# Chunk results turned by VectorE and scaled by a spread row, in a sketched-attention and squared-ReLU kernel

## The chip, the cores and the metric

The kernel runs on one core of one Trainium2 chip. The metric is the time of one execution on the device in microseconds (us). TensorE (PE in the profile) multiplies matrices, VectorE (DVE) and ScalarE (ACT) work element by element and read the matmul results, GpSimd (POOL) works on the on-chip memory only, and SyncE (SP) issues nearly all DMAs. Each engine takes its own instructions in order; semaphores tie the engines together.

## What is computed

Attention with a polynomial sketch comes first, then a feed-forward layer with a squared ReLU. Cut to what matters:

```
phi(x) = outer(S1 x, S2 x)                # 8 x 8 = 64 features for each token and head
kv  = phi(k)^T v ;  z = sum phi(k)        # for each batch and head
x   = (phi(q) kv) / (phi(q) z + 1e-6)     # B*S = 4 * 1088 tokens, H*D = 128 wide
out = relu(x @ w_in)^2 @ w_out            # 128 -> 2048 -> 128, float32
```

The output has 4352 rows of 128 float32, one row for each token.

## The kernel before

**The chunks.** Each of the 4 batches has 1088 tokens: 1024 are cut into two groups of 512 (g = 0, 1), and the 64 that remain are put together over the batches. The feed-forward layer runs over ten chunks in this order: batch 0's first group as two halves of 256 tokens; then (0,1), (1,0), (1,1), (2,0), (2,1), (3,0), of 512 tokens each, (b,g) being batch and group; then the 256 remaining tokens; and (3,1) at the end. For a chunk, `x` is kept transposed and in 16 bits (`xT`, features on partitions, tokens along the free axis). `normalize` (lines 416 to 478) divides each token's 128 values by their largest, so that they fit 16 bits, and leaves the square of that factor in `beta`, a tile of 128 partitions x 4 with token 128 t + p at partition p, column t. GpSimd writes `beta` (line 468).

**One block.** `block` (line 694) does one of 16 slices of the hidden layer: a matmul into `pg` (line 679), the ReLU on ACT into `gt` (line 686), the square on VectorE into `g2` (line 687; the profile names the tile `g`), and two blocks later the matmul that adds into `po` (line 706). `po` is [128 features x 512 tokens]. The tiles `po` have two buffers in PSUM, and so have `pg` and the tiles tagged `ms`.

**The end of a chunk.** `po` has features on the partitions and the output has tokens as rows. So `to_tokens` (line 617) copies `po` to `oT` on ACT (line 620), and two blocks later TensorE transposes it in four 128 x 128 matmuls against the identity into `o_ps` (line 624). `store` (line 648) scales on VectorE with `beta`, one scale for each partition and group of 128 columns, into `o_sb` (line 653), and issues the stores on SP (line 661). For chunk (0,1), whose tokens lie as TensorE transposed them, that is one DMA; for the other five it is four, each with runs of 512 bytes. The last chunk has its own way (lines 715 and 637) and is not touched.

**The other work.** Attention for the next chunks is written as generators (`q_gen`, `k_gen`, and so on), which `pump` advances between blocks. In each batch's turn of the main loop (line 791) there are 16 blocks while `q_gen(b, 1)` and `k_gen(b+1)` run, then the loads for batch b+2 are issued (lines 806 to 813), then 16 blocks while `q_gen(b+1, 0)` runs. The loads of k, v and q of batch b+2 are `pinned`: each stays behind whatever DMA was written just before it for SP. v comes in 32 small DMAs with runs of 128 bytes (line 110). Two tiles of k and of q for the batches 2 and 3 are transposed in blocks of 32 x 32 by VectorE (`turned`, line 237). Up to line 789 the order of the work is written out by hand; behind that, all instructions that are not pinned are put in order for each engine at build time, by what they depend on and by planned times, and so an instruction of a later generator can stand well ahead of its place in the code. At run time the order on an engine is fixed.

Of the kernel before, what the change touches and what calls it, by code (L numbers as in the profile page):

```python
# [8 lines left out]
F32 = mybir.dt.float32  # L9
# [3 lines left out]
def _v(t: bass.AP, off: int, free, p0: int = 0, n: int = 128):  # L13

    p = list(t.ap)[0]
    return bass.AP(
        t.tensor, t.offset + p0 * p[0] + off, [[p[0], n]] + [list(d) for d in free]
    )
# [3 lines left out]
def kernel(  # L22
# [11 lines left out]
    nc = tc.nc  # L34

    B, H, S, D = 4, 4, 1088, 32
    DFF, NC = 2048, 16
    E = 128
    NJ = 8
# [4 lines left out]
    mult = mybir.AluOpType.mult  # L44
# [6 lines left out]
    apool = ctx.enter_context(tc.tile_pool(name="attn", bufs=2))  # L51
    fpool = ctx.enter_context(tc.tile_pool(name="ffn", bufs=3))
    pspool = ctx.enter_context(
        tc.tile_pool(name="psm", bufs=2, space=bass.MemoryType.PSUM)
    )

    def evict(eng, dst, src):
# [422 lines left out]
    chunks = []  # L480
    BY_PE = ((0, 1), (B - 1, 1))

    def chunk_of(b, g, xT, beta):
        at = out.offset + (b * S + 4 * g) * E
        if (b, g) in BY_PE:
            dsts = [(bass.AP(out.tensor, at, [[NJ * E, 128], [1, 512]]), 0, 128, 0, 512)]
        else:
            dsts = [
                (
                    bass.AP(  # L490
                        out.tensor, at + j * E, [[NJ * E, 32], [32 * NJ * E, 4], [1, E]]
                    ),
                    32 * j, 32, 0, 512,
                )
                for j in range(4)
            ]
        chunks.append((xT, 4, [(beta, 4)], dsts))

    def half_gen(phT, t0, m, tag, bufs):

# [8 lines left out]
    def x_gen(b, g, phT, m=32):  # L509
        nd = numerators(b, phT, m)  # L510
        yield 1
        xT = apool.tile([128, 512], F16, name="xT", tag="xT", bufs=3)
        beta = yield from normalize(nd, 4, xT, 0)
        chunk_of(b, g, xT, beta)
        yield 1
# [101 lines left out]
    def to_tokens(po, nt):  # L617

        oT = fpool.tile([128, 512], F32, tag="oT", bufs=2)
        nc.scalar.copy(oT[:, 0:nt], po[:, 0:nt])  # L620
        yield 2
        o_ps = pspool.tile([128, 512], F32, tag="ms", bufs=2)
        for t in range(nt // 128):
            nc.tensor.transpose(  # L624
                o_ps[:, 128 * t : 128 * t + 128], oT[:, 128 * t : 128 * t + 128], iden[:, :]
            )
        return o_ps

    def store_gen(po, nt, betas, dsts):
        o_ps = yield from to_tokens(po, nt)  # L630
        store(o_ps, betas, dsts)

# [15 lines left out]
    def store(po, betas, dsts):  # L648

        o_sb = fpool.tile([128, 512], F32, tag="o_sb", bufs=2)  # L650
        t0 = 0
        for beta, n in betas:
            nc.vector.tensor_tensor(  # L653
                out=_v(o_sb, 128 * t0, [[128, n], [1, 128]]),
                in0=_v(po, 128 * t0, [[128, n], [1, 128]]),
                in1=_v(beta, 0, [[1, n], [0, 128]]),
                op=mult,
            )
            t0 += n
        for dst, p0, n, c0, w in dsts:  # L660
            nc.sync.dma_start(dst, _v(o_sb, c0, [[E, w // E], [1, E]] if n == 32 else [[1, w]], p0, n))

    LOOK = 2
    LAST = 9
# [27 lines left out]
    po = [None]  # L692

    def block():
# [29 lines left out]
        if c0 + n == NC:  # L724
            if ci < LAST:
                stores.append([store_gen(po[0], nt, *chunks[ci][2:]), now[0]])
                pump_stores()
            else:
                _, _, [(beta, _)], [(dst, _, _, _, _)] = chunks[ci]
                store_last(po, beta, dst)  # L730
# [126 lines left out]
```

## Time and profile before

| what | us |
|---|---|
| runs of the kernel before | 213.95, 214.51, 216.04 (median 214.51) |
| the profiled execution: its own time | 213.53 |
| the profiled execution: span of the trace | 211.4 |
| TensorE busy | 201.1 |
| VectorE busy | 145.3 |
| ScalarE busy | 111.7 |
| GpSimd busy | 46.7 |

The span runs from the first to the last instruction in the trace; 2.1 us of the profiled execution's own time lie around it. The granted clock of TensorE is full throughout. In the chain of work that ended last, each line is the piece of work that released the next one; a piece of TensorE work in it can only be shortened by doing less of it or by doing it sooner. In a timeline, brackets give the idle time of an engine before an instruction and what ended it. SPq is SyncE's sequencer, where a DMA's issue takes time.

### The profile page before, as it was taken

The page shows a single profiled execution, that of the slowest core. Times are in us where ns is not written, and L with a number is a line of the kernel's source. Part 1 is how long each engine was busy: PE and PEld are TensorE (multiplying, and loading weights), DVE is VectorE, ACT ScalarE, POOL GpSimd, SP SyncE. Part 2 cuts the span into 40 slices and gives each one's busy share as a digit, 9 for nine tenths or more (in the row PEclk, how much of TensorE's full clock was granted, in tenths as well). Part 3 has the DMA queues.
Part 4 walks back from the last instruction along what each step waited for, and adds up shares of the span by engine and source line. Part 5 has one row for each costly group of instructions (what it writes and reads, how often), then busy time and mean ns, then how long its engine had stood idle before and what let it go on. Part 6 is the DMA issues. An engine that isn't in the chain of part 4 may idle for free.

```text
span 211.4 us, 5449 instructions
## 1 busy us (share of the span) xinstructions
PE 201.1 (95%) x2241; PEld 125.6 (59%) x2241; DVE 145.3 (69%) x281; ACT 111.7 (53%) x212; POOL 46.7 (22%) x66
## 2 busy tenths in 40 slices
PE   7887999899999999999999999999999899999993
PEld 6665778664644544555545555455445454789992
DVE  3667677836586899867777657567858777766662
ACT  3466664254556455455455553655565456555550
POOL 1002174104040683004130971022102210000000
PEclk9999999999999999999999999999999999999999
DMA  6999101422400421231000200001000100010001
GB/s 173 234 349 300 19 2 39 121 34 31 136 0 0 140 47 29 33 110 50 3 2 2 54 3 3 0 15 38 0 0 5 47 3 0 2 50 16 12 0 50
DMA packets 25736, 11.36 MB, mean 54 GB/s; under 512 B 13296, under 2 KB 25328, under 8 KB 25712
## 3 DMA queue, kind: packets, MB, share of 16 engines
q1 hardware_dynamic: 25632, 11.02, 19.8%
q8 instruction: 17, 0.28, 0.6%
q14 instruction: 7, 0.06, 0.1%
q10 hardware_dynamic: 80, 0.01, 0.0%
HBM read 8.79 MB, written 2.23 MB: 52 GB/s over the span
## 4 chain that ended last, share of the span: by engine, by line
PE 84%; DMA 7%; DVE 5%; SPq 2%; issue 1%; ACT 0%; DVEq 0%
PE po L706 47%; PE pg L679 14%; PE po L716 7%; DMA t<-in_k_dram 4%; PE nd L204 4%; PE ab_ps L204 3%; PE t_ps L376 3%; DVE g L687 3%; DMA v_first<-in_v_dram 2%; PE kv_ps L299 2%; PE o_ps L624 2%; PE xt_ps L218 1%; SPq L79 1%; PE x_ps L474 1%; SPq L149 1%
## 5 line engine op out<-in xcount | busy, mean ns | idle before, releaser
L687 DVE TENSOR_TENSOR g<-gt 128x512 f32<-128x512 f32 x136 | 101.6, 757 | 45.6 <-ACT gt L686 42.8
L706 PE MATMUL po<-g,w_o 128*128 128x512 f32 (+1 forms) x288 | 123.4, 525 | 1.2 <-DVE g L687 1.2
L686 ACT ACTIVATE gt<-pg 128x512 f32<-128x512 f32 x136 | 81.2, 599 | 48.3 <-PE pg L679 46.7
L706 PEld LDWEIGHTS po<-g,w_o 128*128 128x128 f32 x288 | 52.3, 191 | 26.3 <-issue 8.8
L241 POOL TENSOR_TENSOR ph<-ab 128x512 f32<-128x512 f32 (+1 forms) x27 | 32.7, 1238 | 62.5 <-ACT ab L59 62.5
L679 PE MATMUL pg<-xT,w_in 128*128 128x512 f16 x112 | 42.5, 381 | 0.0
L679 PEld LDWEIGHTS <-w_in 128*128 128x128 f16 x160 | 15.6, 99 | 20.3 <-issue 16.7
L465 POOL TENSOR_SCALAR mp<-mm 128x4 f32<-128x4 f32 (+2 forms) x11 | 5.3, 487 | 60.3 <-DVE mm L445 60.3
L716 PEld LDWEIGHTS po<-w_o,g 128*128 128x128 f32 x128 | 16.6, 191 | 0.6
L716 PE MATMUL po<-w_o,g 128*128 128x128 f32 x128 | 16.6, 275 | 0.0
L59 ACT COPY sb<-t_ps 128x512 f32<-128x512 f32 (+1 forms) x18 | 9.1, 516 | 9.9 <-PE t_ps L376 9.8
L59 ACT COPY ab<-ab_ps 128x256 f32<-128x256 f32 (+1 forms) x19 | 6.3, 339 | 12.9 <-PE ab_ps L204 11.3
L204 PEld LDWEIGHTS ab_ps<-w_bd,xt 128*32 128x32 f32 (+1 forms) x476 | 8.9, 113 | 6.6 <-issue 3.8
L204 PE MATMUL ab_ps<-w_bd,xt 128*32 128x64 f32 (+1 forms) x476 | 12.1, 224 | 0.2 <-ACT xt L59 0.2
L204 PEld LDWEIGHTS nd<-kvbd,sb 128*32 128x32 f32 x480 | 8.0, 110 | 6.3 <-issue 4.0
L376 PEld LDWEIGHTS t_ps<-iden,ph 128*128 128x128 f32 x60 | 7.5, 141 | 6.8 <-issue 4.9
L204 PE MATMUL nd<-kvbd,sb 128*32 128x66 f32 x480 | 9.9, 222 | 0.9 <-issue 0.9
L477 ACT COPY xT<-x_ps 128x512 f16<-128x512 f16 x7 | 4.1, 586 | 9.9 <-PE x_ps L474 9.9
L376 PE MATMUL t_ps<-iden,ph 128*128 128x128 f32 x60 | 9.2, 272 | 0.0
L59 ACT COPY xt<-xt_ps 128x512 f32<-128x512 f32 (+1 forms) x11 | 5.1, 471 | 6.0 <-PE xt_ps L218 6.0
L653 DVE TENSOR_TENSOR o_sb<-o_ps,beta 128x512 f32<-128x512 f32 (+2 forms) x10 | 5.5, 555 | 3.1 <-PE o_ps L624 2.9
L679 PE MATMUL pg<-xT_h,w_in 128*128 128x256 f16 x32 | 6.0, 273 | 0.9 <-ACT gt L686 0.5
(70 smaller groups left out, 117.2 us busy)
## 6 DMA issues: line engine op xcount, KB each, us to landing
t<-in_k_dram SPq DMA_DIRECT2D x3, 512.0 KB, 4.1
t<-in_q_dram SPq DMA_DIRECT2D x3, 512.0 KB, 4.1
out_dram<-o_sb SPq DMA_DIRECT2D x20, 64.0 KB, 1.8
w_in<-in_moe_w_in_dram SPq DMA_DIRECT2D x2, 512.0 KB, 5.7
w_o<-in_moe_w_out_dram SPq DMA_DIRECT2D x2, 512.0 KB, 7.9
v_turned<-in_v_dram SPq DMA_DIRECT2D x64, 16.0 KB, 1.7
k_sb<-in_k_dram SPq DMA_DIRECT2D x2, 256.0 KB, 3.0
q_sb<-in_q_dram SPq DMA_DIRECT2D x2, 256.0 KB, 5.4
```

What stands on the lines that cost most here:

```text
L59: return nc.scalar.copy(dst, src)
L204: nc.tensor.matmul(out_ps[p0 + c : p0 + c + m, c0 : c0 + w], lhsT[:, l0 + c : l0 + c + m], rhs,)
L241: eng.tensor_tensor(out=_v(ph, 256 * t0, [[64, 4 * w], [8, 8], [1, 8]]), in0=_v(ab, 64 * t0, [[16, 4 * w], [1, 8], [0, 8]]), in1=_v(ab, 64 ...
L299: nc.tensor.matmul(self.ps[c : c + self.m, at : at + w], _v(ph, c0 + 128 * pr + c, [[1, self.m]], p0, n), v_of(2 * pr + c // 64), start=c ...
L376: nc.tensor.transpose(t_ps[:, 128 * t : 128 * t + 128], ph[:, 256 * t + 128 * pr : 256 * t + 128 * pr + 128], iden[:, :],)
L465: nc.gpsimd.tensor_scalar(out=mp[:, 0:T], in0=mm[:, 0:T], scalar1=1.0 / 1024.0, scalar2=None, op0=mult)
L653: nc.vector.tensor_tensor(out=_v(o_sb, 128 * t0, [[128, n], [1, 128]]), in0=_v(po, 128 * t0, [[128, n], [1, 128]]), in1=_v(beta, 0, [[1, n ...
L679: nc.tensor.matmul(pg[:, nt * i : nt * i + nt], w_in[:, 128 * (c + i) : 128 * (c + i) + 128], xT[:, 0:nt],)
L686: nc.scalar.activation(gt[:, :], pg[:, :], Relu)
L687: nc.vector.tensor_tensor(out=g2[:, :], in0=gt[:, :], in1=gt[:, :], op=mult)
L706: nc.tensor.matmul(po[0][:, 0:nt], w_o[:, 128 * c : 128 * c + 128], g2[:, nt * i : nt * i + nt], start=(c == 0), stop=(c == NC - 1),)
L716: nc.tensor.matmul(po[t // 2][:, 128 * (t % 2) : 128 * (t % 2) + 128], g2[:, 128 * t : 128 * t + 128], w_o[:, 128 * c : 128 * c + 128], st ...
```

## The change

For the six chunks (0,1) to (3,0) of 512 tokens, the result is no longer transposed by TensorE. It is scaled while features are still on the partitions, and VectorE transposes it within blocks of 32 x 32. The scales are then needed along the free axis, the same row on all 128 partitions. So `beta` is written to a row of 512 values in DRAM (`line`: 128 x 4 single values of 4 bytes) and read back onto all partitions (`on_all`, 128 times the same 2 KB). Both DMAs are issued on SP where the chunk is put on the list, in `chunk_of`. After the transpose in blocks, a token's 128 features lie in four partition groups of 32, so a store takes 32 partitions and 128 columns and writes runs of 128 bytes: 16 DMAs for a chunk. `oT`'s copy on ACT, the four transposes on TensorE and the use of an `ms` buffer go away for these chunks. The two halves, the remaining tokens and the last chunk are left as they were. `BY_PE` still says which chunks have their q transposed by TensorE, and now also which order the tokens have in the stores.

```
     def chunk_of(b, g, xT, beta):
         at = out.offset + (b * S + 4 * g) * E
-        if (b, g) in BY_PE:
-            dsts = [(bass.AP(out.tensor, at, [[NJ * E, 128], [1, 512]]), 0, 128, 0, 512)]
-        else:
-            dsts = [ ( bass.AP(out.tensor, at + j * E, [[NJ * E, 32], [32 * NJ * E, 4], [1, E]]),
-                    32 * j, 32, 0, 512, ) for j in range(4) ]
-        chunks.append((xT, 4, [(beta, 4)], dsts))
+        if (b, g) == (B - 1, 1):
...
+            return
+        line = dram.tile([1, 512], F32, name="line", tag="line")
+        on_all = apool.tile([128, 512], F32, name="on_all", tag="on_all")
+        nc.sync.dma_start(
+            bass.AP(line.tensor, line.offset, [[1, 128], [128, 4]]), beta[:, 0:4]
+        )
+        nc.sync.dma_start(
+            on_all[:, :], bass.AP(line.tensor, line.offset, [[0, 128], [1, 512]])
+        )
+        step_t, step_u = (E, 32 * NJ * E) if (b, g) in BY_PE else (32 * NJ * E, E)
+        dsts = [
+            ( bass.AP( out.tensor, at + t * step_t + 32 * e,
+                    [[NJ * E, 32], [step_u, 4], [1, 32]], ),
+                32 * e, 32, 128 * t, 128, )
+            for t in range(4)
+            for e in range(4)
+        ]
+        chunks.append((xT, 4, on_all, dsts))
...
+    def turn_gen(po, on_all, dsts):
+        sc = fpool.tile([128, 512], F32, name="sc", tag="oT", bufs=2)
+        nc.vector.tensor_tensor(out=sc[:, :], in0=po[:, :], in1=on_all[:, :], op=mult)
+        yield 1
+        o_sb = fpool.tile([128, 512], F32, name="o_sb", tag="o_sb", bufs=2)
+        nc.vector.transpose(out=o_sb[:, :], in_=sc[:, :])
+        for dst, p0, n, c0, w in dsts:
+            nc.sync.dma_start(dst, _v(o_sb, c0, [[32, w // 32], [1, 32]], p0, n))
+
     def store_gen(po, nt, betas, dsts):
+        if not isinstance(betas, list):
+            yield from turn_gen(po, betas, dsts)
+            return
         o_ps = yield from to_tokens(po, nt)
         store(o_ps, betas, dsts)
```

Both new tiles, `line` and `on_all`, have two buffers; `sc` takes the buffers of `oT`.

More of the change, by code (lines that the diff above doesn't have):

```diff
@@ L54 @@
         tc.tile_pool(name="psm", bufs=2, space=bass.MemoryType.PSUM)
+    )
+    dram = ctx.enter_context(
+        tc.tile_pool(name="dram", bufs=2, space=bass.MemoryType.DRAM)
     )
@@ L484, in chunk_of @@
         at = out.offset + (b * S + 4 * g) * E
-        if (b, g) in BY_PE:
-            dsts = [(bass.AP(out.tensor, at, [[NJ * E, 128], [1, 512]]), 0, 128, 0, 512)]
-        else:
[L488 to L496, printed above, removed]
-        chunks.append((xT, 4, [(beta, 4)], dsts))
+        if (b, g) == (B - 1, 1):
+            dst = bass.AP(out.tensor, at, [[NJ * E, 128], [1, 512]])
+            chunks.append((xT, 4, [(beta, 4)], [(dst, 0, 128, 0, 512)]))
+            return
[6 more added lines that the diff above has]
+            on_all[:, :], bass.AP(line.tensor, line.offset, [[0, 128], [1, 512]])
+        )
+        step_t, step_u = (E, 32 * NJ * E) if (b, g) in BY_PE else (32 * NJ * E, E)
+        dsts = [
+            (
+                bass.AP(
+                    out.tensor, at + t * step_t + 32 * e,
+                    [[NJ * E, 32], [step_u, 4], [1, 32]],
+                ),
+                32 * e, 32, 128 * t, 128,
+            )
+            for t in range(4)
+            for e in range(4)
+        ]
+        chunks.append((xT, 4, on_all, dsts))
     def half_gen(phT, t0, m, tag, bufs):
@@ L660, in store @@
         for dst, p0, n, c0, w in dsts:
-            nc.sync.dma_start(dst, _v(o_sb, c0, [[E, w // E], [1, E]] if n == 32 else [[1, w]], p0, n))
+            nc.sync.dma_start(dst, _v(o_sb, c0, [[1, w]], p0, n))
     LOOK = 2
```

## The prediction

> **What bounds the kernel now.** I read the page's first part, then the chain of work that ended last in order of time, then the timelines of SP, VectorE and GpSimd where the chain bends. Busy times first:
>
> ```profile
> PE 201.1 (95%) x2241; PEld 125.6 (59%) x2241; DVE 145.3 (69%) x281; ACT 111.7 (53%) x212; POOL 46.7 (22%) x66
> ```
>
> TensorE is the bound: only its own work, or a hole of its own, is worth time. The chain at the end of chunk (0,1):
>
> ```profile
> 68.31 0.86 PE po L706 x2
> 69.17 0.44 PE o_ps L624 x4
> 69.61 0.58 PE ab_ps L204 x32
> 70.19 0.34 PE pg L679
> 70.53 0.06 issue
> 70.58 0.61 ACT gt L686
> ```
>
> The four transposes to be removed lie on the chain, 0.44 us, with TensorE's work straight before and behind. The same piece is at 94.40, 115.13, 139.87, 161.46 (0.45) and 183.32. Only at 161.46 does the chain leave TensorE at once:
>
> ```profile
> 161.46 0.45 PE o_ps L624 x4
> 162.19 0.69 DVE o_sb L653
> 163.19 1.08 DVE xs L459
> 164.27 1.49 DVE g L687
> 165.79 1.13 PE po L706 x2
> ```
>
> There VectorE is late, and TensorE stands 0.84 before 165.79. Groups of instructions by shape give the durations:
>
> ```profile
> L237 DVE STREAM_TRANSPOSE xt<-t 128x512 f32<-128x512 f32 x9 | 6.2, 699 | 0.3 <-DMA t<-in_k_dram 0.3
> L653 DVE TENSOR_TENSOR o_sb<-o_ps,beta 128x512 f32<-128x512 f32 x6 | 4.2, 692 | 0.2
> L620 ACT COPY oT<-po 128x512 f32<-128x512 f32 x6 | 3.5, 586 | 1.6 <-PE po L706 1.6
> ```
>
> SP's timeline shows where the new DMAs must stand:
>
> ```profile
> 34.94 0.36 SPq L661 DMA_DIRECT2D out_dram<-o_sb  x1
> 35.40 0.38 SPq L79 DMA_DIRECT2D t<-in_k_dram  x1
> 35.83 17.51 SPq L110 DMA_DIRECT2D v_turned<-in_v_dram  x32
> 53.44 0.39 SPq L79 DMA_DIRECT2D t<-in_q_dram  x1
> ```
>
> and all engines' timeline what hangs on the second of these lines:
>
> ```profile
> 37.41 0.48 POOL L468 TENSOR_TENSOR beta<-mp 128x4 f32<-128x4 f32 x1
> 39.55 0.71 DVE L237 STREAM_TRANSPOSE xt<-t 128x512 f32<-128x512 f32 x1 [0.31 <-DMA t<-in_k_dram]
> 40.75 0.70 DVE L237 STREAM_TRANSPOSE xt<-t 128x512 f32<-128x512 f32 x1
> 41.38 0.42 DVE L60 COPY kvbd<-kv_ps 64x66 f32<-64x66 f32 x2
> 42.49 0.42 PE L204 MATMUL nd<-kvbd,sb 128*32 128x66 f32 x7 [0.90 <-issue]
> ```
>
> Batch 2's k, issued at 35.40, is transposed by VectorE the moment it lands; the copies of kvbd stand behind it, and TensorE waits 0.90 for them.
>
> **Part 1, TensorE.** Six times four transposes: 5 x 0.44 + 0.45 = 2.65 us off the chain. This is the gain; bounds 0 (all of it turned into waits) and 2.65. ACT loses six copies of 0.59, off the chain: nothing.
>
> **Part 2, VectorE.** The scaling stays (0.69: one PSUM and one SBUF operand, as line 653), but two blocks sooner, when `po` ends; a transpose of 0.70 comes on top: 4.2 us in all. Its `o_sb` also has to wait for 16 older stores; the nearest row is GpSimd's copy of `v_turned`, with four semaphore instructions of 0.04 each, so 0.17. The room at (0,1), from VectorE's timeline: idle 0.65 before 68.18, the 0.69 of `o_sb` at 69.70, idle 0.83 before 71.22, less the 0.44 by which all moves up: 1.73, against 0.69 + 0.70 + 0.17 = 1.56. It fits, barely. The same gaps stand at (1,0) and (1,1), nearly so at (2,0). But squares beside GpSimd's work take 1.16 there instead of 0.69, and then nothing is caught up: I charge 0.1 at each of five ends, 0.5 (bounds 0 and 5 x 0.44 = 2.2). At (2,1) VectorE has no gap from 159.57 to 166.9: the 0.44 is not gained, and the transpose may delay `g` by its 0.70. Bounds 0 and 1.1; if the transpose is put behind the squares, in the gap of 1.57 before 168.51, it costs nothing. I take 0.5.
>
> **Part 3, SP.** 96 stores instead of 21, and 12 DMAs for the scales. A store here takes SP 0.43 at the median, a `v_turned` DMA of the same shape 17.51 / 32 = 0.55: 16 take 7 to 9 us, in a chunk's 21 us. No buffer needs them sooner: `o_sb` comes round after two chunks. The last 16 start near 184 and end near 193, before the final stores at 207.9. They cover themselves; without that cover, 1 us for each two stores. In transfer time they are little: from 116 us on the DMA engines are 5% busy.
>
> The spread of scales makes SP wait twice in a row: `line` for `beta`, `on_all` for `line` to land. A store lands 1.6 to 4.1 us after issue (median 1.8) and a 256 KB load like `on_all` in 3.0. `line` has 512 pieces of 4 bytes, which no row shows; by number of pieces it is nearest to the first loads of k (512 pieces, 3.0), by bytes to the stores. I take 2.0. It is needed only at a chunk's end, 8 us or more after `beta`.
>
> What stands behind it on SP counts. The loads for batch b+2 are pinned behind the DMA written before them, which will be `on_all` of (0,1) and of (1,1). So k of batch 2 waits for `beta` at 37.9, 2.0 for `line`, 0.45 for `on_all`: issued at 40.4, not 35.40, landing near 44.5 and not 39.5. v follows until 58.3 (landed at 60.0; GpSimd copies it at 60.17, with nothing else to do until 70.77), q until 58.8. For batch 3, 16 stores of (0,1) and then `beta` of (1,1) at 84.5 come first: k at 87 instead of 70.87, v until 106 (copied at 106.12, nothing behind until 116.72), q landing at 111 (transposed at 118.26). All have cover but one: VectorE's transposes of k. Where they stand in its fixed order is made new at build time. Moved behind the kvbd copies they free TensorE's hole: down to -0.9. Left at their place VectorE stands 5 us, less some 0.65 by which squares are early: +4.3. With the order made for the later load, and TensorE's pieces pulled together, I take 0 between.
>
> On pieces of 4 bytes the Trainium skill (DMA: Bandwidth & Descriptors, Rules for kernel authors) speaks against this change: a last dimension that isn't contiguous becomes one descriptor per element. With the 10.5 ns per packet that its section Bandwidth names for another path, an estimate for 512 in a row is 5.4 us more until `line` lands, and k would land near 50 instead of 44.5, up to 5 us more in the bad case. The trace's 512 pieces in 3.0 us speak against that.
>
> **The sum.** -2.65 + 0.5 + 0.5 + 0 = -1.65. The profiled execution is 213.53 (span 211.4 + 2.1 around it) and becomes 211.9; it lies 0.98 under the median of the runs shown, so for the median 214.51 - 1.65 = 212.9.
>
> **The rivals.** A: the sum above.
> B, the slower side: VectorE is held at k's transposes. For it: they start 0.31 late already now, at the landing, so any error of the planned landing becomes a wait; two more transfers stand in that chain, one of a kind not in the trace. Against: k's product is needed only at 69.54, so there is room to put them later. Price: 4.3 of wait, so 214.51 - 1.65 + 4.3 = 217.2. It decides over 1% once the wait is above 1.65 + 2.1 = 3.8 us.
> C: the transposes go behind the kvbd copies and VectorE's ends of chunks all fit. -2.65 - 0.9 = -3.55: 211.0. For it: TensorE's 0.90 at 42.49 is a wait for VectorE alone.
> D: VectorE becomes the bound at each end of a chunk and eats the gain: 2.65 less 2.2 less 1.1, so +0.65 at most: 214.5 to 215.2. For it: margins of 0.17 us; against: the scaling now comes two blocks sooner.
>
> **How the numbers follow.** A measurement of this kernel can tell about 1% (2.1 us) from no change. Chances: A 0.40 (of it 0.11 faster by over 1%, 0.26 within, 0.03 slower), B 0.25 (0.05 within, 0.20 slower), C 0.20 (0.19 faster, 0.01 within), D 0.15 (0.01, 0.13, 0.01). Faster 0.31, within 0.45, slower 0.24. The range goes from C's 211.0 with 0.4 for the spread of runs, 210.6, to B's 217.2. A's own range is 211.0 to 214.1.
>
> **What would show it.** No 0.44 pieces of line 624 at the six ends, and the next block's `pg` earlier by as much (part 1). VectorE's transposes of `o_sb` with squares behind them on time, and the hole before the `po` after (2,1) at 0.84 to 1.5 (part 2). On SP `line`, then `on_all` 2 us later, then k near 40.4; VectorE without a wait for k over 1 us (part 3). I am wrong if that wait is several us, if `line` takes over 4 us to land, or if the order of TensorE's attention work between the blocks changes so that new holes of over 1 us appear.

## The result and the profile after

| | before | after |
|---|---|---|
| median of 6 runs, us | 214.59 (213.86 to 216.04) | 231.6 (228.8 to 239.06) |
| ratio to before, 95% interval | 1 | 1.074 [1.068, 1.080] |
| profiled execution, us | 213.53, span 211.4 | 233.95, span 232.1 |

The change makes the kernel 7.4% slower, outside the predicted range. Ratios, here and in the experiments, leave out runs at a lower granted clock, here the profiled one and that of 239.06 (0.953 and 0.954 against 0.963 to 0.970 in the other four), so the trace shows a loss of 20.7 us where 7.4% are 15.9. One part of the difference in the trace is a stretch of halved clock at 19 us, which the kernel before does not have there and which costs about 1.7 us.

First the page of after: the row of busy times, the granted clock in 40 slices of 5.8 us, and the engines' shares of the chain that ended last.

```profile
PE 208.0 (90%) x2217; PEld 127.2 (55%) x2217; DVE 147.4 (64%) x287; ACT 108.9 (47%) x206; POOL 46.6 (20%) x66
...
PEclk9997999959799999995999999999999999999998
...
PE 65%; DMA 20%; DVE 8%; issue 2%; SPq 2%; ACT 1%; POOL 1%; DVEq 0%; another core or an unknown queue 0%
```

TensorE has 24 matmuls less and is yet 6.9 us longer busy, because it worked at half clock for a while. A fifth of the chain is now DMA. Which DMA, the table of issues says (KB each, then median us from issue to landing):

```profile
on_all<-line SPq DMA_DIRECT2D x6, 256.0 KB, 6.9
out_dram<-o_sb SPq DMA_DIRECT2D x96, 16.0 KB, 1.5
...
line<-beta SPq DMA_DIRECT2D x6, 2.0 KB, 8.1
```

The smallest transfer of the kernel takes longest: 2 KB in 8.1 us. That is the median of the three landings that the profile could pair; by SP's timeline `on_all`, which waits for `line`, starts 8.1 to 9.9 us after it at all six. The chain shows where that falls (start, us, what):

```profile
39.38 0.49 POOL beta L472
39.86 0.02 issue
39.88 8.36 DMA line<-beta
48.23 0.02 issue
48.25 0.33 SPq L499
...
48.67 7.91 DMA t<-in_k_dram
...
57.24 0.67 DVE xt L241
...
136.59 0.86 PE po L739 x2
137.44 0.58 PE ab_ps L208 x32
```

Before 48.25 SP waits for `line`; then it issues `on_all` and at 48.67 k of batch 2, which was issued at 35.40 in the kernel before. The last two lines are the end of chunk (1,1): `po` is followed by other work at once, and the piece of 0.44 for the transposes is gone, there and at the other five ends. So the gain was had. SP's own timeline:

```profile
39.88 0.37 SPq L496 DMA_DIRECT2D line<-beta  x1
48.25 0.33 SPq L499 DMA_DIRECT2D on_all<-line  x1
48.67 0.40 SPq L83 DMA_DIRECT2D t<-in_k_dram  x1
49.13 19.17 SPq L114 DMA_DIRECT2D v_turned<-in_v_dram  x32
```

What the other engines did meanwhile, from the timeline of all engines and, for the second spread, of TensorE:

```profile
43.31 0.24 PE L208 MATMUL nd<-kvbd,sb 128*32 128x66 f32 x1
...
48.27 0.99 PE L208 MATMUL nd<-kvbd,sb 128*32 128x66 f32 x7 [4.72 <-issue]
...
48.92 0.46 DVE L64 COPY kvbd<-kv_ps 64x66 f32<-64x66 f32 x2 [6.87 <-remote]
...
56.61 1.30 DVE L241 STREAM_TRANSPOSE xt<-t 128x512 f32<-128x512 f32 x2 [6.91 <-DMA t<-in_k_dram]
...
58.87 2.66 PE L739 MATMUL po<-g,w_o 128*128 128x512 f32 x4 [2.87 <-DVE g L720]
...
98.31 1.23 PE L303 MATMUL kv_ps<-v_main,ph 128*32 128x33 f32 x120
105.71 0.37 PE L303 MATMUL kv_ps<-v_main,ph 128*32 128x33 f32 x8 [6.16 <-issue]
```

The second and the last line are the surprise. TensorE stops in the middle of a row of equal matmuls, for nothing that the profile names, and goes on when `line` lands (48.23; and 105.60, from the chain). The 6.91 on VectorE is the wait that rival B spoke of; the 2.87 is what TensorE sees of it.

Where the 20.7 us of span came from can be read at the chunk ends. The time at which ACT (before) or VectorE (after) begins to read the finished `po`:

| chunk | (0,1) | (1,0) | (1,1) | (2,0) | (2,1) | (3,0) | end |
|---|---|---|---|---|---|---|---|
| before | 67.06 | 92.29 | 113.02 | 137.75 | 158.45 | 181.19 | 211.4 |
| after | 80.38 | 115.54 | 135.71 | 160.01 | 180.27 | 202.72 | 232.1 |
| after less before | +13.3 | +23.3 | +22.7 | +22.3 | +21.8 | +21.5 | +20.7 |

All is lost at two places, and from then on 2.6 us are won back in five steps: the prediction's gain. At the first place: hole 4.72, wait for `g` 2.87, half clock (the clock's records show 0.5 from 46.4 to 53.2 and from 60.0 to 63.4): of these TensorE worked 4.9 and 3.4 us, and half of each is lost, 2.5 and 1.7; with the 1.7 of the stretch at 19 us, 13.5 of the 13.3. Of the 4.72, though, 0.90 stood at the same place in the kernel before (42.49 there), so the terms that are new come to 12.6. At the second: hole 6.16, wait for `g` 1.00, half clock from the hole's end at 105.7 to 111.2, 2.8: 10.0 of the 9.9.

### The profile page after: what moved, and what is told of

It reads as the page before. It is cut to its first block, busy times and chain, and to the rows that moved or that the text cites. A ratio compares the mean times of both kernels' runs of the same rounds, so it can differ in the third digit from the quotient of the medians.

```text
span 232.1 us, 5517 instructions
## 1 busy us (share of the span) xinstructions
PE 208.0 (90%) x2217; PEld 127.2 (55%) x2217; DVE 147.4 (64%) x287; ACT 108.9 (47%) x206; POOL 46.6 (20%) x66
## 4 chain that ended last, share of the span: by engine, by line
PE 65%; DMA 20%; DVE 8%; issue 2%; SPq 2%; ACT 1%; POOL 1%; DVEq 0%; another core or an unknown queue 0%
PE po L739 38%; PE pg L712 11%; DMA t<-in_k_dram 10%; DMA line<-beta 8%; PE po L749 6%; PE nd L208 3%; DVE g L720 3%; PE ab_ps L208 2%; PE t_ps L380 2%; DMA v_first<-in_v_dram 2%; ACT gt L719 1%; PE xt_ps L222 1%; SPq L83 1%; PE kv_ps L303 1%; DVE xt L241 1%
## 5 line engine op out<-in xcount | busy, mean ns | idle before, releaser
L739 PE MATMUL po<-g,w_o 128*128 128x512 f32 (+1 forms) x288 | 130.2, 551 | 5.3 <-DVE g L720 5.3
L720 DVE TENSOR_TENSOR g<-gt 128x512 f32<-128x512 f32 x136 | 100.3, 748 | 43.5 <-ACT gt L719 40.8
L739 PEld LDWEIGHTS po<-g,w_o 128*128 128x128 f32 x288 | 55.1, 201 | 32.9 <-DVE g L720 13.2
L712 PE MATMUL pg<-xT,w_in 128*128 128x512 f16 x112 | 43.3, 388 | 0.0
L712 PEld LDWEIGHTS <-w_in 128*128 128x128 f16 x160 | 16.0, 101 | 21.9 <-issue 18.3
L208 PE MATMUL nd<-kvbd,sb 128*32 128x66 f32 x480 | 10.4, 223 | 4.8 <-issue 4.7
L481 ACT COPY xT<-x_ps 128x512 f16<-128x512 f16 x7 | 4.1, 585 | 22.3 <-PE x_ps L478 22.3
L241 DVE STREAM_TRANSPOSE xt<-t 128x512 f32<-128x512 f32 x9 | 6.1, 696 | 10.3 <-DMA t<-in_k_dram 10.3
L64 DVE COPY kvbd<-kv_ps 64x66 f32<-64x66 f32 (+1 forms) x7 | 1.6, 234 | 16.5 <-PE kv_ps L303 9.6
L63 ACT COPY ab<-ab_ps 128x256 f32<-128x256 f32 (+1 forms) x19 | 6.3, 339 | 10.8 <-PE ab_ps L208 10.5
L303 PE MATMUL kv_ps<-v_main,ph 128*32 128x33 f32 x384 | 4.2, 199 | 6.2 <-issue 6.2
```

The lines of the kernel that those rows point to most:

```text
L63: return nc.scalar.copy(dst, src)
L208: nc.tensor.matmul(out_ps[p0 + c : p0 + c + m, c0 : c0 + w], lhsT[:, l0 + c : l0 + c + m], rhs,)
L241: nc.vector.transpose(out=xt[:, :], in_=_v(src, 128 * g, [[NJ * D, 4], [1, 128]]))
L303: nc.tensor.matmul(self.ps[c : c + self.m, at : at + w], _v(ph, c0 + 128 * pr + c, [[1, self.m]], p0, n), v_of(2 * pr + c // 64), start=c ...
L712: nc.tensor.matmul(pg[:, nt * i : nt * i + nt], w_in[:, 128 * (c + i) : 128 * (c + i) + 128], xT[:, 0:nt],)
L720: nc.vector.tensor_tensor(out=g2[:, :], in0=gt[:, :], in1=gt[:, :], op=mult)
```

## The experiments

The theory after the result: `line` is slow because its pieces of 4 bytes are neighbours in DRAM, and while it is in flight other things in the chip stand as well. Rivals: the wait of SP behind it is all; the 16 stores or VectorE's new transposes have their share; the second DMA (`on_all`, 256 KB) is at fault.

**1. Without the spread.** The change, with `on_all` replaced by a tile of ones.

```
-        line = dram.tile([1, 512], F32, name="line", tag="line")
-        on_all = apool.tile([128, 512], F32, name="on_all", tag="on_all")
-        nc.sync.dma_start(bass.AP(line.tensor, line.offset, [[1, 128], [128, 4]]), beta[:, 0:4])
-        nc.sync.dma_start(on_all[:, :], bass.AP(line.tensor, line.offset, [[0, 128], [1, 512]]))
+        on_all = ones_all
```

> The changed kernel without line and on_all: the six chunks are multiplied by a tile of ones made once at the start, so this kernel leaves the scaling of their results out; the multiplication itself, the transposes by VectorE and the 96 stores stay. Theory 1 (all of the loss comes from the spread of scales by way of DRAM): TensorE keeps its 2.65 us and little is lost at the chunks' ends, so 211 to 213.5 us, clock 1.00 all through. Theory 2 (the stores in runs of 128 bytes, 96 DMAs on SP, cause a good part of it): 220 to 230 us. Theory 3 (VectorE's six extra transposes hold up the squares): above 216 us.

Measured: 211.31, ratio 0.986 [0.979, 0.992]. So the two DMAs are the whole loss, and the rest of the change, in a kernel that leaves the scaling of these results out, is worth 2.7 us, as TensorE's 2.65 said.

**2. The line alone,** added to the kernel before; nothing reads it and SP does not wait for its landing.

```
+        if (b, g) != (B - 1, 1):
+            line = dram.tile([1, 512], F32, name="line", tag="line")
+            nc.sync.dma_start(bass.AP(line.tensor, line.offset, [[1, 128], [128, 4]]), beta[:, 0:4])
```

> The kernel before, and on top the six line DMAs of 512 pieces of 4 bytes to DRAM, issued at the same place on SP; nobody waits for them and nobody reads them. Theory 1a (while such a DMA waits to land, an instruction fetch doesn't complete, and TensorE stands when it has run out of instructions): TensorE gets holes of 3 to 6 us that end with the landing of line, one or two of them as in the changed kernel (4.7 and 6.2 us), and the clock halves for 6.8 us behind each: 220 to 230 us. Theory 1b (the loss comes only from SP, which stands 8 us before on_all, so that the loads of k come late): SP waits for nothing here, so 214 to 215.5 us, and no holes.

Measured: 242.91, ratio 1.133 [1.127, 1.139], well above the 220 to 230 that I expected. More is lost than in after, with 12 KB written and no wait of SP. This fells the rival that SP's wait is all. TensorE's part of the timeline:

```profile
41.40 1.13 PE L715 MATMUL po<-g,w_o 128*128 128x256 f32 x4
47.69 0.27 PE L208 MATMUL nd<-kvbd,sb 128*32 128x66 f32 x1 [5.15 <-issue]
52.92 0.65 PE L208 MATMUL nd<-kvbd,sb 128*32 128x66 f32 x7 [4.97 <-issue]
```

and the table of waits (us in total, times, longest):

```profile
DVE xt L241 <- DMA t<-in_k_dram: 21.9, 2, 11.4
...
PE kv_ps L303 <- issue: 11.6, 2, 5.9
PE nd L208 <- issue: 10.1, 2, 5.2
```

The profile pairs one landing of `line`, the last, after 10.5 us; by the semaphore's updates in the trace the other five come after 8.2 to 9.5. k, issued straight behind it, lands after 12.7. TensorE has holes of 21.7 us in all, and VectorE waits 21.9 for k.

**3. Line and `on_all`,** both unread, added to the kernel before.

```
+            nc.sync.dma_start(bass.AP(line.tensor, line.offset, [[1, 128], [128, 4]]), beta[:, 0:4])
+            nc.sync.dma_start(on_all[:, :], bass.AP(line.tensor, line.offset, [[0, 128], [1, 512]]))
```

> The kernel before, and on top both DMAs of the spread, line and on_all, which nobody reads: TensorE still transposes the results. Theory 1 (the spread is the whole loss): the changed kernel's 231 plus the 2.65 us that TensorE does not save here, 228 to 235 us, with VectorE waiting 3 to 7 us for k of batch 2. Theory 2 or 3 (stores or VectorE's transposes): close to 214.5 us.

Measured: 242.04, ratio 1.130 [1.122, 1.139], more than I expected. The same as `line` alone, so `on_all` and SP's wait for `line` together change nothing on balance. With SP waiting, VectorE waits for k 10.3 instead of 21.9, but TensorE's holes remain (4.7 in `nd`, 10.8 in `kv_ps`).

**4. The line in runs of 128 bytes.** The whole change, but VectorE first transposes `beta` in blocks, and `line` is written in 16 pieces of 128 bytes by four DMAs.

```
+        nc.vector.transpose(out=beta_t[b % 2][:, 32 * g : 32 * g + 32], in_=beta[:, :])
+        for e in range(4):
+            nc.sync.dma_start(
+                bass.AP(line.tensor, line.offset + 32 * e, [[128, 4], [1, 32]]),
+                _v(beta_t[b % 2], 32 * g, [[1, 32]], 32 * e, 4),
+            )
```

> The changed kernel, but beta is transposed within 32 by VectorE first (a tile of 128 x 32, about 0.2 us for each chunk) and written to line in 16 pieces of 128 bytes by 4 DMAs instead of 512 pieces of 4 bytes. Theory 1 with the small pieces as its cause: line lands in about 2 us, no hole in TensorE above 1.5 us, clock near 1.00: 211 to 215 us. If the way through DRAM itself is slow (any write to DRAM followed by a read of it): line again takes 6 us or more and the time stays above 224 us.

Measured: 213.44 over 10 runs, ratio 1.000 [0.995, 1.004]; the clock is full throughout. SP's timeline:

```profile
38.93 0.63 SPq L499 DMA_DIRECT2D line<-beta_t  x2
40.51 0.36 SPq L503 DMA_DIRECT2D on_all<-line  x1
40.97 0.45 SPq L83 DMA_DIRECT2D t<-in_k_dram  x1
41.46 17.77 SPq L114 DMA_DIRECT2D v_turned<-in_v_dram  x32
59.33 0.39 SPq L83 DMA_DIRECT2D t<-in_q_dram  x1
```

The prediction had k at 40.4, v until 58.3 and q at 58.8. With a line that lands in time the change does what was forecast of SP, and VectorE waits for k 1.1 us in all. This version has the change's plan with another size of piece, and the 7.4% are gone.

**5. The line spread out.** As 2, but each value 512 bytes from the next.

```
-                bass.AP(line.tensor, line.offset, [[1, 128], [128, 4]]), beta[:, 0:4]
+                bass.AP(line.tensor, line.offset, [[128, 128], [128 * 128, 4]]), beta[:, 0:4]
```

> As the kernel before with six unread line DMAs of 512 pieces of 4 bytes, but each value goes 512 bytes from the next one in DRAM instead of beside it. If line is slow to land because neighbouring values (32 of them in 128 bytes, written by different DMA engines) have to be merged one after the other in the same piece of memory: it lands in 2 to 3 us, TensorE has no holes, 214 to 216 us. If 512 pieces of 4 bytes are slow wherever they go: 8 us or more again, and 230 to 245 us.

Measured: 220.44, ratio 1.028 [1.021, 1.035], between the two ranges that I had named; the landing was forecast, what remains was not. 512 pieces of 4 bytes as before, and `line` lands after 2.0 us (at most 2.1) instead of 8.2 to 10.5. So neither the number of pieces nor their size alone makes it slow: that they are neighbours does. What remains goes with k, which is issued at 39.48 behind `line`, which waits for `beta`:

```profile
DVE xt L241 <- DMA t<-in_k_dram: 7.0, 2, 4.6
...
PE nd L208 <- issue: 3.3, 1, 3.3
```

The hole lies at 42.69 to 46.03, when `line` (landed at 41.03) is no longer in flight. With one stretch of 6.8 us at half clock, in which up to 3.4 are lost, it comes to at most 6.7 us, against 6.1 measured.

**6. Both DMAs issued by GpSimd** instead of SP, in the changed kernel.

```
-        nc.sync.dma_start(
+        nc.gpsimd.dma_start(
```

> The changed kernel with line and on_all issued by GpSimd instead of SP, so that the loads of k, v and q do not stand behind them on SP. Theory 1a (completions of other transfers are held while line is in flight): VectorE's waits for k are gone (10.3 us in the changed kernel, worth some 4 us on TensorE), but TensorE's holes at an instruction fetch stay and so does the halved clock: 221 to 228 us. Theory 1b (only SP's order matters): 212 to 215 us.

Measured: 231.33, ratio 1.065 [1.058, 1.072], which is some 228 us, at the upper end of the 221 to 228 that I expected. VectorE no longer waits for k, so the loads on SP are free of `line`. But `line` still takes 10.1 us to land (the median of the three that the profile pairs), TensorE still has its holes, and now GpSimd stands instead of SP:

```profile
POOL on_all L499 <- DMA line<-beta: 38.1, 4, 10.7
...
POOL on_all L499 <- issue: 18.9, 2, 10.1
...
PE kv_ps L303 <- issue: 6.4, 2, 4.0
```

**7. Sixteen stores of 128-byte runs,** in the kernel before.

```
-                        out.tensor, at + j * E, [[NJ * E, 32], [32 * NJ * E, 4], [1, E]]
+                        out.tensor, at + j * E + 32 * e, [[NJ * E, 32], [32 * NJ * E, 4], [1, 32]],
...
+                for e in range(4)
```

> The kernel before, but for the five chunks that are stored by four DMAs with runs of 512 bytes, 16 DMAs with runs of 128 bytes, as in the change. TensorE still transposes and the scales stay per partition. Theory 1: nothing, 213.5 to 215 us. Theory 2 (small stores cost): above 217 us.

Measured: 214.11, ratio 1.000 [0.997, 1.004]. The stores cost nothing, as predicted.

**8. Scaling after the transpose, without DRAM.** VectorE transposes `po` first; then a token's scale is on its partition again, and the same `beta` serves, laid out over 16 columns by GpSimd.

```
+        sc = fpool.tile([128, 512], F32, name="sc", tag="oT", bufs=2)
+        nc.vector.transpose(out=sc[:, :], in_=po[:, :])
...
+            in0=_v(sc, 0, [[128, 4], [32, 4], [1, 32]]),
+            in1=_v(on_all, 0, [[1, 4], [4, 4], [0, 32]]),
```

> No way through DRAM at all: VectorE transposes po within 32 first and scales after it, when a token's four groups of features lie on four partition groups, with beta laid out as 128 x 16 by 16 small multiplications on GpSimd (about 0.1 to 0.2 us each, 2 to 3 us for each chunk, beside GpSimd's 9 us of idle time). If the spread was the whole loss, this keeps what the ones on all partitions showed: 210 to 213 us, 0.5 to 1.5% under the kernel before. If the small GpSimd work holds up VectorE or the layout costs more than the spread in runs of 128 bytes: 213.5 us or more.

Measured: 211.61, ratio 0.987 [0.982, 0.991], 1.3% faster than the kernel before. The groups by shape:

```profile
L471 POOL TENSOR_TENSOR beta<-mp 32x4 f32<-32x4 f32 x96 | 28.6, 298 | 5.7
L651 DVE STREAM_TRANSPOSE sc<-po 128x512 f32<-128x512 f32 x6 | 4.3, 709 | 0.0
L654 DVE TENSOR_TENSOR o_sb<-sc,beta 128x512 f32<-128x512 f32 x6 | 4.1, 681 | 0.0
```

The idea behind the change holds: the span of the trace falls by 2.8 (211.4 to 208.6), for 28.6 us of work on GpSimd, which has the room.

**9. The program shifted.** 32 small matmuls more at the start of the changed kernel, which become 128 more of TensorE's records, to see whether the holes are tied to a place in its program.

```
-    idle_products(256, 256, 128)
+    idle_products(256, 256, 128, *([2] * 32))
```

> The changed kernel with 32 tiny matmuls of zeros more at the very start (a weight load and a matmul each, 64 instructions of TensorE, some 2 us at most), so that all later pieces of TensorE's program that are fetched begin 64 instructions sooner. In the changed kernel TensorE stopped in the middle of a run of 128 equal matmuls, behind the 120th, for 6.16 us, while line of (1,1) was in flight. If what TensorE waits for is the next piece of its program: it now stops behind the 88th (64 instructions are 32 matmuls with their weight loads), again until line has landed. If it waits for a buffer, a semaphore or the memory: the break stays at 120, or sits at the run's ends.

Measured in a single run: 256.78, some 25 us above after, of which the added matmuls themselves explain little. The break did not come at the place that I had named. The first hole moved from `nd`, which now runs without a stop, into `kv_ps`, 74 records sooner in the same work, and the second row of `kv_ps` is whole. From the timelines of TensorE and ACT:

```profile
52.27 1.17 PE L303 MATMUL kv_ps<-v_main,ph 128*32 128x33 f32 x112
58.27 0.48 PE L303 MATMUL kv_ps<-v_main,ph 128*32 128x33 f32 x16 [4.83 <-issue]
...
109.96 1.30 PE L303 MATMUL kv_ps<-v_main,ph 128*32 128x33 f32 x128
...
118.55 0.27 ACT L481 COPY xT_rem<-x_ps 128x128 f16<-128x128 f16 x1 [5.49 <-remote]
...
119.37 0.58 PE L712 MATMUL pg<-xT,w_in 128*128 128x512 f16 x1 [4.15 <-ACT gt L719]
```

**10. Pieces of 16 bytes.** In the changed kernel the four values of a partition stand together in DRAM, and VectorE reads `on_all` with a step of four.

```
-            bass.AP(line.tensor, line.offset, [[1, 128], [128, 4]]), beta[:, 0:4]
+            bass.AP(line.tensor, line.offset, [[4, 128], [1, 4]]), beta[:, 0:4]
```

> The changed kernel, but line keeps the order of beta in memory: each partition writes its four values side by side, 128 pieces of 16 bytes, and VectorE reads on_all with a step of 4 in the scaling. A quarter of the pieces, 8 neighbours in 128 bytes instead of 32. If each neighbour's merge adds its share (6.1 us over 2.0 for 512 pieces): line lands in 3.5 us and the time is 213 to 218 us. If any piece under some larger size costs the same whole wait: 8 us, and 227 to 233 us.

Measured: 217.13, ratio 1.012 [1.006, 1.018]. `line` lands after 1.4 us, faster than I expected, and most of the loss is gone with two access patterns changed and nothing else. Left are waits for k of 4.2 us, a hole of 1.7 and 3.4 us at half clock.

**11. A quarter of the line.** As 2, but one column of `beta`: 128 neighbouring pieces of 4 bytes.

```
-                bass.AP(line.tensor, line.offset, [[1, 128], [128, 4]]), beta[:, 0:4]
+                bass.AP(line.tensor, line.offset, [[1, 128], [128, 1]]), beta[:, 0:1]
```

> The kernel before with six unread line DMAs that write one column of beta only: 128 neighbouring pieces of 4 bytes. It leaves three quarters of line out. If the merges follow one another over the whole row: 2.0 + 6.1 / 4 = 3.5 us to land. If only the pieces in the same 64 or 128 bytes wait for one another, and different ones run side by side: about 8 us as with 512 pieces.

Measured in a single run: 245.36, as slow as the whole line:

```profile
DVE xt L241 <- DMA t<-in_k_dram: 21.4, 2, 11.0
...
PE kv_ps L303 <- issue: 11.5, 2, 5.9
PE nd L208 <- issue: 10.1, 2, 5.2
```

By the semaphore's updates three of its six flights end after 7.7 to 8.4 us, with all 16 updates in the trace. A quarter of the pieces costs the same, so it is no fixed time for each piece of one row.

**What the holes are.** Two things were counted in the traces. First, the landings: the records of `line`'s 512 pieces in after lie between 40.79 and 41.16, and yet the semaphore gets its last update at 48.23. Until then the DMA engines are nearly idle. A transfer of 16 KB on the queue that the profile calls "instruction" takes 0.9 to 1.4 us in the kernel before. In after, three that lie within a flight of `line` take 3.6 to 3.8 (at 41.7, 100.2 and 180.4 us), one beside `on_all` and k takes 4.1 (49.3), and the other thirteen 0.9 to 1.4, two of them (140.7, 153.5) also within a flight, near its end and near its start. Second, the place: there are 17 such transfers in a run of some 4,500 records of TensorE, one for each 260, and where nothing stands they start within some 100 records of the same place, so I read them as TensorE's program. TensorE stops for `nd` before its record 1217 in every kernel but 9, the kernel before included: for 0.5 to 0.9 us there and in kernels 1, 4, 6, 7 and 8, for 1.7 in kernel 10, 3.3 in kernel 5, and 4.7 to 5.0 in after and in kernels 2, 3 and 11 (2 and 11 also stop one or two records earlier); in 2, 3 and 11 the next stop is before record 2277. It goes on 1.2 to 1.6 us after the program transfer nearest to that place has ended, in ten of these twelve kernels; in after and in kernel 3 it goes on 2.7 and 2.8 us after it, with the landing of `line`. In kernels 2, 5 and 11 that transfer starts only while TensorE stands at record 1217. And kernel 9, with the program shifted, has no stop for `nd`. All this speaks for a program that comes late. In the four other flights of `line` in after TensorE has no gap of over 0.3 us.

Against it as the whole cause stand TensorE's semaphore updates. In after the last two products for `kv_ps` end at 41.96 and 42.32 by the trace and are told at 48.74 and 48.90, which is what VectorE's 6.87 before `kvbd` waits for. In kernels 2, 3 and 11 the same two are told 6.3 to 7.5 us late, and in kernel 9 five updates come within 0.15 us, at 118.53 to 118.68 with the landing of `line`, for matmuls that ended between 113.0 and 115.2. In the kernel before and in kernel 5 these updates come within 0.1 us. So kernel 5, whose `line` has landed by then, has the late program without late updates, and after and kernels 2, 3 and 11 have both. What holds either of them isn't settled; that `line`'s flight is behind the loss is, by kernels 1, 2, 4, 5 and 10.

## Why the prediction was wrong

**The step that failed** is in Part 3: "`line` has 512 pieces of 4 bytes, which no row shows; by number of pieces it is nearest to the first loads of k (512 pieces, 3.0), by bytes to the stores. I take 2.0." It took 8.1 to 9.9 us (8.2 to 10.5 in kernel 2). The bounds of 1.6 to 4.1 came from stores with runs of 512 bytes and more, the 3.0 from loads in pieces of 512 bytes, and kernels 5 and 10 show that pieces far apart, or of 16 bytes, do land in 1.4 to 2.0. None of those rows has the property that mattered, small pieces side by side in DRAM. I had named 4 us as the point at which I am wrong, but gave nothing beyond it a chance, so the range ended at 217.2.

From the wrong term two things followed that the sum had no terms for. k was issued at 48.67 instead of 40.4 and VectorE waited 6.9 and 3.4 us for it, the mechanism of rival B. That its price of 4.3 is near what TensorE saw (2.87 + 1.00) is luck: B priced a single wait of 5 us. But most of the loss is TensorE's own: holes of 4.72 and 6.16 and 7.0 us lost to halved clock. A DMA was costed by who waits for it; that engines which do not wait for it stand while it is in flight was no case of mine.

**A wait put down to the wrong engine.** The prediction reads TensorE's 0.90 at 42.49 as a wait for VectorE's copies of `kvbd`, and rival C and the bound of -0.9 rest on it. In kernel 4 the copies come ahead of k's transposes and end at 41.03, and TensorE still stands until 42.27. From the timelines of VectorE and TensorE:

```profile
40.57 0.46 DVE L64 COPY kvbd<-kv_ps 64x66 f32<-64x66 f32 x2 [0.40 <-PE kv_ps L303]
...
42.27 0.42 PE L208 MATMUL nd<-kvbd,sb 128*32 128x66 f32 x7 [0.53 <-issue]
```

In after `nd` goes on at 48.27, before the copies at 48.92. It is the stop before record 1217 described above, so there was nothing for VectorE to free. The sum took 0 for this and did not suffer, but the same stop, long, became a main part of the loss.

**The estimate by pieces.** The estimate worked out from the Trainium skill (DMA: Bandwidth & Descriptors, Bandwidth), 5.4 us more, that is 7.4 until landing, was nearer to the 8.1 than mine; I dismissed it by a row of loads. But a time for each piece isn't the cause either: 128 pieces are as slow as 512 (kernel 11), and 512 spread ones take 2.0 (kernel 5). What the Trainium skill says in DMA: Bandwidth & Descriptors, Queues, rings and completion order, fits the late landings: a semaphore's increment is ordered and lands only after every earlier write of that DMA engine, across its queues. In the trace, pieces done at 41.16 are told at 48.23, and k behind `line` takes 12.7 in kernel 2. Why the neighbours' writes are slow is not shown. The same page's Specifications name read-modify-write below 512 bytes; no run here can show it, because the profile's sum of HBM reads counts what the instructions ask for (8.79 MB in the kernel before and in kernel 2, and in after 6 x 256 KB more, just `on_all`).

**What was right.** Part 1: no transposes on the chain, 2.6 us won back after the second loss, 2.7 in kernel 1, against 2.65. Part 2: scaling 0.69 and transpose 0.71 as taken; at (2,1) the wait before `po` is 0.99, inside the 0.84 to 1.5 that I gave:

```profile
185.58 0.38 PE L712 MATMUL pg<-xT,w_in 128*128 128x512 f16 x1
186.95 1.12 PE L739 MATMUL po<-g,w_o 128*128 128x512 f32 x2 [0.99 <-DVE g L720]
```

The five charges of 0.1 can't be told from nothing: kernel 1 is at the full gain. Rival D did not come. In Part 3 the stores (kernel 7) and the whole order on SP (kernel 4) were right, with one reservation: kernel 4 has the same gain on TensorE and yet a ratio of 1.000. Up to the end of chunk (1,0) it is 1.8 us behind the kernel before, at the end level with it. TensorE's waits for `g` of 0.51, 0.62 and 0.66 (at 61.89, 94.14 and 108.64), which the kernel before does not have, say that VectorE is late there. k comes 5.6 us later there than before, for which I took 0; kernel 4 also has six small transposes of VectorE (0.21 each) that the change has not. Which of the two it is wasn't tried.

## What to carry to other kernels

Before a DMA of single values is put into a kernel, look whether the pieces are neighbours in DRAM; if so, turn them on chip first or give each partition 16 bytes or more. Cost a DMA also by what stands while it is in flight, not only by who waits for it, and where no row of the trace has its shape, leave the range open on the side that was never measured. If only a layout is wanted, see whether the order of two steps can be swapped so that it isn't needed (kernel 8).

## What the runs showed of the hardware

- A write of 2 KB to DRAM in neighbouring pieces of 4 bytes lands after 8.1 to 9.9 us in the change and 8.2 to 10.5 in kernel 2; 512 bytes apart after 2.0 (kernel 5); in pieces of 16 bytes after 1.4 (kernel 10). Whether pieces of one or of several DMA engines get in each other's way wasn't tried.
- Behind it, k's load takes 12.7 us instead of 4.1 (kernel 2). While it is in flight, a 16 KB transfer on the queue called "instruction" took up to 3.8 us instead of 0.9 to 1.4, TensorE's semaphore told of finished products 6.6 to 6.8 us late, and in two of its six flights TensorE stopped, for 4.7 and 6.2 us (all in the change).
- From within each of these holes the granted clock was 0.5 for 6.8 us, which cost 2.5 and 2.8 us, so a hole costs about half as much again. The Trainium skill (TensorE: Matmul & The Clock Gate, What's actually happening) gives windows of about 3.4 us for both ways; the stretches here, 3.4 and 6.8 us, and 10.2 and 13.7 where two holes follow each other (kernels 2 and 11), are one to four of these.
- VectorE's transpose of 128 x 512 takes 0.71 us from PSUM (kernel 8), as from SBUF (0.70).
